# A recurrence beside a full attention: the new memory turned on VectorE instead of TensorE, its inputs loaded as tokens, the five instruction orders set anew

## The chip, the cores and the metric

The kernel runs on one core of one Trainium2 chip. The metric is the device time of one execution in microseconds; three runs of the kernel before gave 1315.05, 1323.09 and 1323.85 us, with a median of 1323.09 us. One more execution was profiled, and all durations come from it.

## The reference

Two attentions over the same kind of input are mixed by a gate. Part A is a recurrence over 64 segments of 32 tokens: each segment is preceded by 8 memory rows, and the first 8 rows of its output are the memory of the next segment. Part B is ordinary softmax attention with 32 heads of 18 elements over 2048 tokens.

```python
for s in range(n_seg):                       # 64 segments, one after the other
    xs = x[:, s * seg_len:(s + 1) * seg_len, :]
    h = jnp.concatenate([mem, xs], axis=1)   # 8 + 32 rows of 576
    q, k, v = (einsum('btd,dhe->bhte', h, W) for W in (Wq, Wk, Wv))   # 32 heads of 128
    p = softmax(where(mask, q @ k^T * scale, -1e9))
    o = einsum('bhte,hed->btd', p @ v, Wo)
    mem = o[:, :M, :]                        # M = 8
    outs.append(o[:, M:, :])
# b = softmax attention of B_x with wqkv and wo;  g = sigmoid((x * gate_w).sum(-1))
out = g * a + (1 - g) * b
```

B_x is given, but the mix uses A_x for both parts.

## The kernel before, in words

**How the work is laid out.** The kernel lists some 8,600 operations with `add(name, engines, cost, function, dependencies, ...)`; each function issues a handful of instructions. The order of the operations on each engine is written out by hand in `ORDER` (L16): one list for each of TensorE (PE), VectorE (DVE), ScalarE (ACT), GpSimd (POOL) and SyncE (SP), as steps from one operation's number to the next. Every engine works through its list strictly in order. `FULL` (L309) names the products that run untiled where two forms are possible. `Plan.run` (L424) only merges the five lists into one program with the help of the costs, and picks zero products (below).

**Stages.** First x is transposed on TensorE (`xt`, L717) into xT, and the projections of part B follow (`pq` L870, `pv` L908), while the weights of part A are loaded from the POOL queue (L807, L812). Then two things run interleaved until the end. Part B is 512 visits: a visit is four row-tiled score products (`sb`, L1065), two exponentials on ScalarE (L1074, L1078) and four column-tiled value products (`ob`, L1088). Part A is the 64 segments: projections Q, K, V (L1437, six results of four chunks each, and a tail that two results share, `T`), evictions on VectorE (32x32 block transposes L1478, casts L660), copies into `qk` and `v_sb` on POOL or VectorE (L1522, L1502), scores (L1544), exponential (L1554), sums and their reciprocals (L1570, L1582, L1590), the weighted values (`po`, L1612), evictions into `ot`, and the output product in two halves (`op0`, `op1`, L1319). Queries, keys and values of the last 8 tokens of each segment don't depend on the memory and are made ahead (`la`, L1156 and L1160, stores `ls`). At the end the output product of part B (`pfx`, L1831) and the gate's mix follow.

**From one segment to the next.** Half 0 of the output product is summed on VectorE (L1346). When half 1 is done, VectorE adds the two into `obf` as 128 partitions by 144 columns, bfloat16 (`oc`, L1645). TensorE turns the memory rows of it by 16 small products with slices of the identity (`fo`, L1660 and L1667), and VectorE copies the result into columns 0 to 7 of `ht` (`ph`, L1676). The other 24 columns of `ht` are the segment's tokens: POOL copies them (`lh`, L1386) from `xg`, which is loaded for four segments at a time (`lx`, L1380) from `xtd`, a copy of xT in DRAM stored once (`xs`, L835). The projections of the next segment wait for both copies. Features stand in `ht` as four chunks of 128 rows and a fifth with the 4 x 16 left over; the weights are loaded in the same order of rows (`row0`, `rows`).

**Zero products.** Between the first and the last value product of a visit group the planner looks at how long TensorE would wait for its next operation. From about 0.3 us on it puts four zero-weight products of 512 columns there (or one untiled), which add nothing to the open accumulator (`warm_col`, `warm_full`, L1036 and L1042).

**Banks and tokens.** The value accumulator `ob` has a PSUM bank of its own and `sb` three; four more (`pb`) are handed round between all others, the fourth score product of a visit, the projections, `acc` of the output product and `pw` of the turned memory among them.

Of the kernel before, what the change touches and what calls it, by code (L numbers as in the profile page):

```python
# [1898 lines left out]
```

## Time and profile before

| | |
|---|---|
| median of 3 runs | 1323.09 us |
| profiled execution, its time | 1319.63 us |
| profiled execution, span of the instructions | 1317.8 us |
| instructions | 72973 |
| HBM read, written | 52.74 MB, 31.12 MB |
| projections of part B end | at about 95 us |
| first segment's projections start | at about 128 us |

Engines in the page: PE is TensorE's products, PEld its weight loads, DVE VectorE, ACT ScalarE, POOL GpSimd, SP the queue of DMA issues. A group's row has the line, engine, operation, output and input tiles, shape and count, then busy us and mean ns of one, then the idle time ahead of it and what ended that. Products are pipelined, so a row's duration is longer than its distance to the next: the distance between starts tells what TensorE really spent.

### The profile page before, as it was taken

Reading aid. Unit: us, or ns where it says so; the run is one execution under the profiler, and the core shown is the slowest. Engines: PE = TensorE matmul, PEld = TensorE weight load, DVE = VectorE, ACT = ScalarE, POOL = GpSimd, SP = SyncE. Lnnn points to the kernel's source line nnn. Section 1 sums busy time; section 2 is a strip of 40 time slices with the busy share of each in tenths; the row PEclk is TensorE's granted clock in tenths of the full one; section 3 lists DMA queues with packets and bytes.
Section 4 is the critical chain, followed back from the end, with each engine's and each line's share of the span. In section 5 each row is a group of like instructions: output and inputs, shape, how many; then the busy total and the mean of one; then the engine's idle time right before and its main releaser. Section 6 shows DMA issues by size and latency. Waiting matters only on the chain.

```text
span 1317.8 us, 72973 instructions
## 1 busy us (share of the span) xinstructions
PE 1287.2 (98%) x32799; PEld 692.9 (53%) x32799; DVE 781.2 (59%) x1778; ACT 1118.5 (85%) x1343; POOL 519.2 (39%) x1291
## 2 busy tenths in 40 slices
PE   8999999999999999999999999999999999999998
PEld 5444544555555555555555545655555444544555
DVE  3234566656566666565656666656666566566667
ACT  3678989978889898888978898898878899998896
POOL 4361353423543246434452445543334343423320
PEclk9999999999999999999999999999999999999999
DMA  8887522011211021111121211121122111111115
GB/s 240 273 287 243 176 48 49 26 31 28 64 40 42 16 47 53 31 31 36 41 49 30 43 38 39 34 49 30 36 49 63 25 23 24 35 38 25 22 51 184
DMA packets 145063, 88.59 MB, mean 67 GB/s; under 512 B 102439, under 2 KB 135383, under 8 KB 144751
## 3 DMA queue, kind: packets, MB, share of 16 engines
q1 hardware_dynamic: 127527, 51.33, 15.2%
q0 software_dynamic: 15088, 30.41, 7.6%
q8 instruction: 256, 4.19, 1.3%
q10 hardware_dynamic: 2136, 2.19, 0.6%
q14 instruction: 56, 0.46, 0.1%
HBM read 52.74 MB, written 31.12 MB: 64 GB/s over the span
## 4 chain that ended last, share of the span: by engine, by line
PE 88%; ACT 4%; DMA 3%; DVE 2%; issue 2%; SPq 1%; DVEq 0%; ACTq 0%
PE pvv L1437 31%; PE acc L1319 12%; PE sb L1065 12%; PE ob L1088 9%; PE pv L1156 5%; PE pso L1612 3%; ACT etb L1074 3%; PE pv L1160 3%; PE pq L870 2%; PE psh L1544 2%; PE prb L1590 2%; PE po L1831 1%; PE psh L1536 1%; PE pw L1660 1%; PE pvb L908 1%
## 5 line engine op out<-in xcount | busy, mean ns | idle before, releaser
L1074 ACT ACTIVATE etb<-sb 128x1536 bf16<-128x1536 f32 x512 | 744.0, 1453 | 118.8 <-PE sp L1065 89.5
L1078 ACT ACTIVATE etb<-sp 128x512 bf16<-128x512 f32 x512 | 306.5, 599 | 0.8 <-PE sp L1065 0.7
L1437 PEld LDWEIGHTS <-ht 128*32 128x32 bf16 (+1 forms) x7680 | 170.6, 94 | 215.4 <-issue 115.8
L1478 DVE STREAM_TRANSPOSE tf<-pvv 128x512 f32<-128x512 f32 x256 | 181.2, 714 | 166.0 <-PE pvv L1437 159.5
L1522 POOL CAST qk<-tf 128x512 bf16<-128x512 f32 x142 | 88.0, 621 | 342.9 <-DVE tf L1478 339.8
L1502 POOL COPY v_sb<-tm 32x256 f32<-32x256 f32 x360 | 147.9, 411 | 153.7 <-DVE tm L660 103.0
L1065 PE MATMUL sb<-qch,kch 32*128 32x512 bf16 x1536 | 202.0, 385 | 5.0 <-ACT etb L1074 1.9
L1065 PE MATMUL sp<-qch,kch 32*128 32x512 bf16 x512 | 196.6, 384 | 2.0 <-DVE vt L660 1.8
L1088 PE MATMUL ob<-etb,vch 128*32 128x512 bf16 x2048 | 194.8, 383 | 1.6 <-issue 0.6
L1437 PE MATMUL pvv<-wk_m,ht 128*32 128x512 bf16 x2048 | 163.2, 381 | 0.2
L1437 PE MATMUL pvv<-wq_m,ht 128*32 128x512 bf16 x2048 | 162.7, 381 | 0.7
L1319 PE MATMUL acc<-wo,ot 128*32 128x288 bf16 (+1 forms) x6144 | 160.2, 248 | 1.1 <-DVE ot L660 0.6
L1437 PE MATMUL pvv<-wv_m,ht 128*32 128x512 bf16 x2048 | 155.2, 380 | 0.2
L1319 PEld LDWEIGHTS <-ot 128*32 128x32 bf16 x6144 | 113.5, 97 | 31.3 <-issue 11.4
L1065 PEld LDWEIGHTS <-kch 32*128 32x128 bf16 x2048 | 56.2, 91 | 121.3 <-issue 107.5
L660 DVE CAST ot<-pso 128x320 bf16<-128x320 f32 x192 | 87.7, 485 | 45.8 <-PE pso L1612 43.9
L660 DVE CAST tm<-pvv 128x512 bf16<-128x512 f32 x101 | 69.2, 687 | 45.2 <-PE pvv L1437 41.8
L1088 PEld LDWEIGHTS <-vch 128*32 128x32 bf16 x2048 | 52.0, 95 | 48.2 <-issue 30.9
L1601 DVE TENSOR_TENSOR et<-et,prb 128x320 bf16<-128x320 bf16 x128 | 62.0, 486 | 23.1 <-PE prb L1590 17.5
L1554 ACT ACTIVATE et<-psh 128x320 bf16<-128x320 f32 x128 | 55.7, 440 | 17.6 <-PE psh L1544 16.4
L660 DVE CAST vl<-pv 128x512 bf16<-128x512 f32 x65 | 44.6, 690 | 40.6 <-PE pv L1156 24.2
L1405 POOL COPY qk<-xl 128x64 f32<-128x64 f32 x256 | 52.2, 244 | 28.4 <-DMA xl<-qkd 8.9
(160 smaller groups left out, 1810.6 us busy)
## 6 DMA issues: line engine op xcount, KB each, us to landing
xl<-qkd SPq DMA_DIRECT2D x32, 256.0 KB
qkd<-vl SPq DMA_DIRECT2D x41, 128.0 KB
wo<-in_A_Wo_dram POOLq DMA_DIRECT2D x8, 576.0 KB, 5.8
wq_m<-in_A_Wq_dram POOLq DMA_DIRECT2D x8, 512.0 KB, 6.8
vgd<-vt SPq DMA_DIRECT2D x32, 128.0 KB
wk_m<-in_A_Wk_dram POOLq DMA_DIRECT2D x8, 512.0 KB, 6.8
wv_m<-in_A_Wv_dram POOLq DMA_DIRECT2D x8, 512.0 KB, 5.7
v_sb<-vld SPq DMA_DIRECT2D x128, 32.0 KB
```

The costliest lines, as they stand in the source:

```text
L660: nc.vector.tensor_copy(out=out_of(), in_=in_of())
L1065: nc.tensor.matmul(sb[:, j, :] if j < 3 else sp[:, :], lhsT=kc[r, o:o + P], rhs=qt_[r, :], start=True, stop=True, tile_position=(32 * j, 0),)
L1074: nc.scalar.activation(out=etb[:, 0:3, :], in_=box["sb", gq, kb][:, :, :], func=ACT.Exp, scale=scale_b)
L1078: nc.scalar.activation(out=etb[:, 3, :], in_=box["sp", gq, kb][:, :], func=ACT.Exp, scale=scale_b)
L1088: nc.tensor.matmul(ob[32 * j:32 * j + 32, :], lhsT=vc[:, o + 32 * j:o + 32 * j + 32], rhs=etb[:, j, :], start=(kb == 0), stop=(kb == NKB - ...
L1156: nc.tensor.matmul(out_, lhsT=lw, rhs=rw, start=(c == 0), stop=(c == NF), skip_group_check=wide)
L1319: nc.tensor.matmul(acc[32 * q:32 * q + 32, :], lhsT=o[:, slot, t0:t0 + CT], rhs=wo[:, h, d:d + n], start=(first and s_ == (s_ % 2 if wide ...
L1437: nc.tensor.matmul(o, lhsT=ht[:, c, :], rhs=rw, start=start, stop=stop, tile_position=(r, 32 * j), skip_group_check=True,)
L1478: nc.vector.transpose(out=tf[:, :], in_=box["pvv", s, n][:, :])
L1502: move(out=out_.bitcast(FP32), in_=in_.bitcast(FP32)) if e == "POOL" else move(out=out_, in_=in_)
L1522: move(out=opened["qk"][:, hf, a, 0:16 * L].rearrange("p (k t) -> p k t", t=L)[:, :, 0:CT], in_=box["tf", s, "QK"[a] + str(hf)][:, :].rear ...
L1601: nc.vector.tensor_tensor(out=et[:, :], in0=et[:, :], in1=box["prb", s, hf][:, :], op=ALU.mult)
```

## The change

It does five things.

1. The fold on TensorE (`fo`) and the copy behind it (`ph`) are gone. While half 1 of the output product runs, VectorE prepares `gs`: the summed half 0, multiplied by a mask that keeps the 8 memory rows, plus the next segment's tokens. After half 1, `gx` multiplies the accumulator by the same mask and adds the prepared rows, into `hn` (128 x 144, bfloat16). `gt` turns columns 0 to 127 of `hn` into `ht` by 32x32 blocks; `gc` (two copies) and `gv` do the same for the 16 left over. `oc` follows `gx`. The four main chunks of a projection wait for `gt`, the shared tails for `gv`.
2. Tokens are loaded as they are, one row of the input after the other (`lx`, four DMAs for four segments, straight from x), into the rows of `xg` where the mask is zero. `xtd`, its stores `xs` and the copies `lh` are gone.
3. The order of features follows from that: row 32g + r of chunk c is feature 144g + 32c + r. x is transposed in 20 column-tiled pieces instead of 5 untiled ones, and weights, gate and tails are loaded in that order; a weight load moves 2048 columns of a row at once, where it moved two pieces of 1024.
4. The zero products are gone, and so is the planner's model of instruction fetches that went with them.
5. `ORDER` and `FULL` are written anew for all engines, and some costs that the planner uses are changed.

The lists themselves, read as operation numbers, hold: TensorE 4501 operations before and 4437 after, VectorE 1684 and 2038, ScalarE 1358 and 1257, POOL 680 and 728, SP 374 and 259.

```diff
 ORDER = {
...
-    LAG = {"SP": 0.66, "ACT": 0.66, "POOL": 1.25}
+    LAGS = ({"SP": 0.8, "ACT": 0.8, "POOL": 2.5}, {"SP": 0.66, "ACT": 0.66, "POOL": 1.25})
...
-    def zeros(self, op, est, mode):
...
     def rows(t, c):
-        return t[row0(c):row0(c) + P, :]
+        return t.rearrange("(g r) n -> g r n", r=RW)[:, 32 * c:32 * c + 32, :]
...
-            for c in range(NF):
-                nc.tensor.transpose(out=ptx[:, c, :], in_=xn[:, row0(c):row0(c) + P], identity=ident[:, :])
...
+            for c in range(NF + 1):
+                for g in range(4):
+                    r = slice(32 * g, 32 * g + 32)
+                    lw = xn[:, RW * g + 32 * c:RW * g + 32 * c + 32] if c < NF else xd[:, r]
+                    nc.tensor.transpose(out=ptx[r, c, :], in_=lw, identity=ident[:, :], tile_position=(0, 32 * g))
...
-    xstores = [store_xt(q) for q in range(NQC)]
...
+    def later_x(s):
+        def ld_x(e):
+            src = x_td[s * seg:(s + 4) * seg, :].rearrange("(i t) d -> t i d", t=seg)
+            for g in range(NF):
+                queue(e)(out=opened["xg"][32 * g + M:32 * g + CT, :, :], in_=src[0:seg - LO, :, RW * g:RW * g + RW])
+
+        return add(f"lx{s}", *carrier(4, s > 0), ld_x, [opening, last_x], dmas=4, kb=110)
+
+    def turned_state(s, deps, state, held):
+        def merge(e):
...
+                nc.vector.scalar_tensor_tensor(
+                    out=hn[:, 0:RW], in0=state["acc"][:, :], scalar=opened["mrow"][:, 0:1], in1=held()[:, RW:2 * RW],
+                    op0=ALU.mult, op1=ALU.add,
+                )
+
+        def swap(e):
+            hn = opened["hn"]
+            for k in range(2):
+                nc.vector.tensor_copy(out=hn[64 * k:64 * k + 64, RW:RW + TR], in_=hn[64 - 64 * k:128 - 64 * k, P:RW])
+
+        def flip(a, b):
+            def fn(e):
+                ht = opened["ht", s % 2][:, :, :].rearrange("p c t -> p (c t)")
+                nc.vector.transpose(out=ht[:, a:b], in_=opened["hn"][:, a:b])
+            return fn
+
+        used = hist.get(s - 2, {}).get("used", ())
+        gx = add(f"gx{s}", "DVE", 0.37, merge, deps)
+        gt = add(f"gt{s}", "DVE", 0.22, flip(0, P), [gx, *used])
+        gc = add(f"gc{s}", "DVE", 0.16, swap, [gx])
+        return gx, gt, add(f"gv{s}", "DVE", 0.11, flip(P, P + 32), [gc, *used])
...
-                        [ops[0]] if c else [h_ready, lh, *weight_loads[("wq", "wk", "wv")[kind]]],
+                        [ops[0]] if c else [h_main, *weight_loads[("wq", "wk", "wv")[kind]]],
...
-            both = add(f"T{names[0]}.{s}", "PE", 0.216, tails, [ops[0] for ops in parts], mode="quad", pairs=8)
+            both = add(f"T{names[0]}.{s}", "PE", 0.216, tails, [h_tail, *(ops[0] for ops in parts)], mode="quad", pairs=8)
...
+            def prepare(e, s=s, st0=first_half):
+                nc.vector.scalar_tensor_tensor(
+                    out=st0["sum"][:, RW:2 * RW], in0=st0["sum"][:, 0:RW], scalar=opened["mrow"][:, 0:1],
+                    in1=opened["xg"][:, (s + 1) % 4, :], op0=ALU.mult, op1=ALU.add,
+                )
...
+        c1 = add(f"oc{s}", "DVE", 0.308, ob_cast, [mids[1], half_sum, nxt], take=("obf",) if s % 4 == 0 else (),
...
-            fo = add(f"fo{s}", "PE", 0.13, fold, [c1], mode="col", take=("pb",), pairs=16, drain=0.245)
...
-            h_ready = add(f"ph{s}", "DVE", psum_copy(40), put_h, [fo, *prev.get("used", ())], give=(("pb", fo, 0),))
```

More of the change, by code (lines that the diff above doesn't have):

```diff
@@ L463, in run @@
                 mode = op.form
-                open_ = (open_ or op in self.opens) and op not in self.closes
-                self.count += op.waits
-                dur += self.fetched(est, dur, pairs)
             op.eng, op.start, op.end = e, est, est + dur
@@ L570 @@
     nc.vector.memset(veil[:], 0.0)
-    nil = const.tile([P, P], BF16, name="nil")
-    nc.vector.memset(nil[:], 0.0)
     nc.vector.memset(bsel[:], 0.0)
@@ L587 @@
     )
-    selm = ident[:, :].rearrange("p (a b t) -> p b a t", a=2, t=32)[:, :, :, 0:M]
-    SL = (0, 2, 1, 3)
     dpool = ctx.enter_context(tc.tile_pool(name="dpool", bufs=1, space=bass.MemoryType.DRAM))
     a_dram = dpool.tile([S, Dm], BF16, name="a_dram")
-    xtd = dpool.tile([(NF + 1) * P, S], BF16, name="xtd")
     qtd = dpool.tile([Dm, S], BF16, name="qtd")
@@ L712, in dup @@
         def dup(e):
-            box["xd", n] = xd = given(pw, "xd", [P, 2, 2, 2 * TR], BF16)
-            tail = box["xn", n][:, :].rearrange("p (b r) -> p b r", r=2 * RW)[:, :, P:P + 2 * TR]
-            nc.vector.tensor_copy(out=xd[:, :, :, :], in_=tail.unsqueeze(1).to_broadcast([P, 2, 2, 2 * TR]))
-        du = add(f"xd{n}", "DVE", 0.2, dup, [ld], take=("xd",))
+            box["xd", n] = xd = given(pw, "xd", [P, 2, 2, 2, TR], BF16)
+            tail = box["xn", n][:, :].rearrange("p (h g r) -> p g h r", h=2, r=RW)[:, :, :, P:RW]
+            nc.vector.tensor_copy(out=xd[:, 0, :, :, :], in_=tail)
+            for h in range(2):
+                nc.vector.tensor_copy(out=xd[:, 1, :, 1 - h, :], in_=tail[:, :, h, :])
+        du = add(f"xd{n}", "DVE", 0.3, dup, [ld], take=("xd",))
         def turn(e):
@@ L1032 @@
     last_vi = last_va = None
-    def warm_col(e):
-        for j in range(4):
-            nc.tensor.matmul(
-                box["ob"][32 * j:32 * j + 32, :], lhsT=nil[:, 0:32], rhs=ident[:, :].unsqueeze(1).to_broadcast([P, 4, P]), start=False, stop=False,
-                tile_position=(0, 32 * j), skip_group_check=True,
-            )
-    def warm_full(e):
-        nc.tensor.matmul(
-            box["ob"][:, :], lhsT=nil[:, :], rhs=ident[:, :].unsqueeze(1).to_broadcast([P, 4, P]),
-            start=False, stop=False, skip_group_check=True,
-        )
-    plan.warm = {"col": warm_col, "full": warm_full}
     for gq in range(GB * NQC):
@@ L1227, with first_mem @@
     opened = {}
+    def first_mem():
+        return opened["ot"][:, :, :].rearrange("p h t -> p (h t)")[:, 0:RW]
     def open_rest(e):
@@ L1262, in load_m0 @@
     def load_m0(e):
-        m0 = opened["ot"][:, :, :].rearrange("p h t -> p (h t)")[:, 0:Dm]
-        dma(out=m0[0:M, :], in_=A_mem0[0])
-        box["m0"] = m0
-    m1 = add("m0", "SP", 0.4, load_m0, [opening], dmas=1, kb=10)
-    def dup_m0(e):
-        m0d = opened["et", 0][:, 0:P].rearrange("p (a b r) -> p a b r", a=2, b=2)
-        tail = box["m0"][0:M, :].rearrange("p (b r) -> p b r", r=2 * RW)[:, :, P:P + 2 * TR]
-        nc.vector.tensor_copy(out=m0d[0:M, :, :, :], in_=tail.unsqueeze(1).to_broadcast([M, 2, 2, 2 * TR]))
-        box["m0d"] = m0d
-    m2 = add("m0d", "DVE", 0.25, dup_m0, [m1])
-    def turn_m0(e):
-        ptm = bank([P, NF + 1, 32], BF16, "ptm")
-        for c in range(NF):
-            nc.tensor.transpose(
-                out=ptm[:, c, 0:M], in_=box["m0"][0:M, row0(c):row0(c) + P], identity=ident[0:M, 0:M]
-            )
-        nc.tensor.transpose(
-            out=ptm[:, NF, 0:M], in_=box["m0d"][0:M, :, :, :].rearrange("p a b r -> p (a b r)"),
-            identity=ident[0:M, 0:M],
-        )
-        box["ptm"] = ptm
-    m3 = add("m0t", "PE", 0.3, turn_m0, [m2], mode="full", take=("pb",), pairs=5)
-    def put_m0(e):
-        ht, ptm = opened["ht", 0], box["ptm"]
-        nc.vector.tensor_copy(out=ht[:, :, 0:M], in_=ptm[:, :, 0:M])
-    h_ready = add("m0h", "DVE", 0.55, put_m0, [m3], give=(("pb", m3, 0),))
+        for g in range(NF):
+            dma(out=first_mem()[32 * g:32 * g + M, :], in_=A_mem0[0][:, RW * g:RW * g + RW])
+    m0 = add("m0", "SP", 1.6, load_m0, [opening], dmas=4, kb=10)
     plan.tokens_of("tm", 2)
@@ L1302 @@
     plan.tokens_of("tf", 2)
-    plan.tokens_of("xg", 1)
     a_stores = {}
@@ L1374 @@
         ht_i = s % 2
-        if s % 4 == 0:
-            def ld_x(e, s=s):
-                box["xg", s // 4] = xg = given(opened["fix"], "xg", [P, NF + 1, P], BF16)
-                src = slice(s * seg, (s + 4) * seg)
-                queue(e)(out=xg[:, :, :], in_=xtd[:, src].rearrange("(c p) t -> p c t", p=P))
-            lx = add(f"lx{s}", *carrier(1, s > 0), ld_x, [opening, xstores[s * seg // QC], prev.get("lh")], take=("xg",), dmas=1, kb=164)
-        def put_x(e, s=s, ht_i=ht_i):
-            ht, xg, t = opened["ht", ht_i], box["xg", s // 4], slice(s % 4 * seg, s % 4 * seg + seg - LO)
-            nc.gpsimd.tensor_copy(out=ht[:, :, M:CT].bitcast(FP32), in_=xg[:, :, t].bitcast(FP32))
-        lh = add(f"lh{s}", "POOL", 0.24, put_x, [lx, *prev2.get("used", ())], give=(("xg", lx, 0),) if s % 4 == 3 else ())
-        cur["lh"] = lh
+        if s == 0:
+            lx = later_x(0)
+            _, h_main, h_tail = turned_state(0, [m0, lx], None, None)
         def ld_l(e, s=s, sq=sq, si=si):
@@ L1508 @@
             pvs.append((
-                add(f"qd{hf}.{s}", ("DVE", "POOL"), (0.8, 0.75), put_v(hf, (1, 3)), before),
-                add(f"qc{hf}.{s}", ("DVE", "POOL"), (0.8, 0.75), put_v(hf, (0, 2)), before),
+                add(f"qd{hf}.{s}", ("DVE", "POOL"), (0.71, 0.87), put_v(hf, (1, 3)), before),
+                add(f"qc{hf}.{s}", ("DVE", "POOL"), (0.71, 0.87), put_v(hf, (0, 2)), before),
             ))
@@ L1527 @@
                 turned.append(add(
-                    f"ct{a}{hf}.{s}", ("POOL", "DVE"), (0.66, 0.45), ct, [ev_a, prev.get(f"psh{hf}")], give=(("tf", ev_a, 0),),
+                    f"ct{a}{hf}.{s}", ("POOL", "DVE"), (0.63, 0.435), ct, [ev_a, prev.get(f"psh{hf}")], give=(("tf", ev_a, 0),),
                 ))
@@ L1574, in sm @@
                         )
-            s_ = add(f"sm{hf}.{s}", "PE", 0.08, sm, [x_],
-                     mode="col", take=("pb",), pairs=12, alt=("full", 0.088, 3), drain=0.218)
+            s_ = add(f"sm{hf}.{s}", "PE", 0.1, sm, [x_],
+                     mode="col", take=("pb",), pairs=12, alt=("full", 0.11, 3), drain=0.218)
             def rc(e, hf=hf, s=s):
@@ L1616, in pso @@
                         )
-            o_ = add(f"po{hf}.{s}", "PE", 0.2, pso, [n_, lv, *pvx], mode="tall", take=("pb", "pb"), pairs=16, waits=0.15, drain=0.26,
+            o_ = add(f"po{hf}.{s}", "PE", 0.25, pso, [n_, lv, *pvx], mode="tall", take=("pb", "pb"), pairs=16, waits=0.15, drain=0.26,
                      give=(("tm", evx, 0),))
@@ L1645, in ob_cast @@
             nc.vector.tensor_tensor(
-                out=opened["obf"][:, s % 4, TR:TR + RW], in0=st["acc"][:, :], in1=st0["sum"][:, 0:RW], op=ALU.add
+                out=opened["obf"][:, s % 4, :], in0=st["acc"][:, :], in1=st0["sum"][:, 0:RW], op=ALU.add
             )
-        c1 = add(f"oc{s}", "DVE", 0.308, ob_cast, [mids[1], half_sum], take=("obf",) if s % 4 == 0 else (),
+        nxt = None
+        if s + 1 < n_seg:
+            def prepare(e, s=s, st0=first_half):
[3 more added lines that the diff above has]
+                )
+            if (s + 1) % 4 == 0:
+                lx = later_x(s + 1)
+            gs = add(f"gs{s + 1}", "DVE", 0.27, prepare, [half_sum, lx])
+            nxt, h_main, h_tail = turned_state(s + 1, [mids[1], gs], acc_state, lambda st0=first_half: st0["sum"])
+            last_x = gs
+        c1 = add(f"oc{s}", "DVE", 0.308, ob_cast, [mids[1], half_sum, nxt], take=("obf",) if s % 4 == 0 else (),
                  give=(("pb", acc_state["op0"], 0), ("sum", sum_op, 0)))
@@ L1685, in st_a @@
                     queue(e)(
-                        out=dst[0:seg - LO, :, RW * SL[j]:RW * SL[j] + RW],
-                        in_=opened["obf"][32 * j + M:32 * j + CT, :, TR:TR + RW],
+                        out=dst[0:seg - LO, :, RW * j:RW * j + RW], in_=opened["obf"][32 * j + M:32 * j + CT, :, :],
                     )
@@ L1818, in mul_a @@
                     nc.vector.tensor_scalar_mul(out=ga_view(n), in0=ares_all[:, n, :], scalar1=gsb[:, n:n + 1])
-            gates[n] = add(f"ga{n}", ("ACT", "DVE"), (act_time(576), 0.65), mul_a, [la, *last["used"]])
+            gates[n] = add(f"ga{n}", ("ACT", "DVE"), (0.77, 0.51), mul_a, [la, *last["used"]])
     HD2 = Dm // 2
@@ L1851 @@
             halves.append(add(
-                f"cb{n}.{hf}", "DVE", psum_copy(288), combine, [a, gates[n]], give=(("pb", a, 0),)
+                f"cb{n}.{hf}", "DVE", 0.518, combine, [a, gates[n]], give=(("pb", a, 0),)
             ))
```

150 lines of the change are left out of this document (51 added, 99 removed), and 583 rows, old and new, of tables (FULL, ORDER).

## The prediction

> **What bounds the kernel now.** I read the page first: busy shares and the chain that ended last.
>
> ```profile
> span 1317.8 us, 72973 instructions
> ...
> PE 1287.2 (98%) x32799; PEld 692.9 (53%) x32799; DVE 781.2 (59%) x1778; ACT 1118.5 (85%) x1343; POOL 519.2 (39%) x1291
> ...
> PE 88%; ACT 4%; DMA 3%; DVE 2%; issue 2%; SPq 1%; DVEq 0%; ACTq 0%
> ```
>
> TensorE is the bound: 98% busy, 88% of the chain. But a product's row is longer than its distance to the next, so that share hides short waits. What TensorE spends must be read from the starts, in the timeline. I took the passage from one segment to the next, because the change sits there; this one is typical.
>
> ```profile
> 402.36 0.30 DVE L1346 TENSOR_TENSOR sum<-acc,sum 64x144 f32<-64x144 f32 x1
> 402.38 0.61 PE L1319 MATMUL acc<-wo,ot 128*32 128x144 bf16 x28
> ...
> 402.81 0.39 PE L1088 MATMUL ob<-etb,vch 128*32 128x512 bf16 x4
> ...
> 403.03 0.39 PE L1036 MATMUL ob<-ident,nil 128*32 128x512 bf16 x4
> 403.04 0.31 DVE L1645 TENSOR_TENSOR obf<-acc,sum 128x144 bf16<-128x144 f32 x1 [0.38 <-PE acc L1319]
> ...
> 403.41 0.22 PE L1660 MATMUL pw<-ident,obf 128*32 128x16 bf16 x8
> ...
> 403.47 0.20 PE L1667 MATMUL pw<-ident,obf 128*32 128x8 bf16 x8
> ...
> 403.61 0.39 PE L1065 MATMUL sb<-qch,kch 32*128 32x512 bf16 x3
> ...
> 403.75 0.20 DVE L1676 CAST ht<-pw 128x40 bf16<-128x40 f32 x1 [0.40 <-PE pw L1667]
> ...
> 403.93 0.43 PE L1088 MATMUL ob<-etb,vch 128*32 128x512 bf16 x4
> ...
> 404.15 1.07 PE L1437 MATMUL pvv<-wv_m,ht 128*32 128x512 bf16 x16
> ```
>
> Prices from these starts. Four column products of 512 take 0.22 us (402.81 to 403.03). The same work followed by another tiling costs more: `sb` at 403.61 to `ob` at 403.93 is 0.32, so **a change of tiling costs 0.10 us**. The fold takes 0.20 up to `sb`, of which 0.10 is such a change: 0.10 of its own. The zero products take 0.22, and TensorE waits another 0.16 for the fold (403.03 to 403.41, less 0.22). The seven rounds of `acc` are 0.0625 apart, so the last starts at 402.76 and the next segment's projections 1.39 later. Read alike for all 63 passages the mean is 1.45 us, 91.4 us in sum: 51.0 useful products, 12.2 changes of tiling, 6.6 fold, 5.0 zero products (23 of them lie here) and **16.6 us of waits**, 8.8 of them just ahead of the fold. The groups agree:
>
> ```profile
> L1660 PE MATMUL pw<-ident,obf 128*32 128x16 bf16 x504 | 14.4, 176 | 1.1 <-issue 0.5 <-DVE obf L1645 0.5
> L1036 PE MATMUL ob<-ident,nil 128*32 128x512 bf16 x212 | 20.2, 379 | 0.0
> L1042 PE MATMUL ob<-ident,nil 128*128 128x512 bf16 x4 | 1.2, 379 | 0.0
> L1660 PEld LDWEIGHTS <-obf 128*32 128x32 bf16 x504 | 8.7, 94 | 23.5 <-DVE obf L1645 21.8 <-issue 0.8
> ...
> PEld L1660 <- DVE obf L1645: 21.8, 53, 0.7
> ```
>
> 504 is 63 folds of 8; 212/4 + 4 makes 57 zero products. The fold's weight loads waited 21.8 us in 53 cases for VectorE's sum; less the 0.22 that the product ahead was still streaming, that is 10 us, close to 8.8.
>
> **The passage after the change.** The chain is now `acc`, `gx`, `gt`, projections. `gx` and `gt` are not in the trace; the nearest rows:
>
> ```profile
> L1645 DVE TENSOR_TENSOR obf<-acc,sum 128x144 bf16<-128x144 f32 x64 | 19.7, 308 | 33.1 <-PE acc L1319 31.6 <-DMA kch<-ktd 1.2
> L1846 DVE SCALAR_TENSOR_TENSOR wk_m<-po,omg,wv_m 128x288 bf16<-128x288 f32 x24 | 12.2, 516 | 2.4 <-PE po L1831 1.1 <-PE po L1835 0.2
> L1131 DVE STREAM_TRANSPOSE stage<-tn 128x512 bf16<-128x512 bf16 x32 | 22.3, 696 | 1.9 <-DMA otd<-stage 1.7
> L660 DVE CAST ot<-pso 128x320 bf16<-128x320 f32 x192 | 87.7, 485 | 45.8 <-PE pso L1612 43.9
> L660 DVE CAST tm<-pvv 128x512 bf16<-128x512 f32 x101 | 69.2, 687 | 45.2 <-PE pvv L1437 41.8
> L1676 DVE CAST ht<-pw 128x40 bf16<-128x40 f32 x63 | 12.5, 199 | 28.4 <-PE pw L1667 28.4
> ```
>
> The two casts give 1.05 ns per column ((687-485)/192). By that `gx` is 516 - 144 x 1.05 = 0.365 us; its bounds are 0.31 (a plain sum of that size) and 0.52 (the 288 columns). `gt` is 696 - 384 x 1.05 = 0.29; its bounds are 0.17 (a quarter of 696) and 0.49 (a cast of 320 columns). I take the slope, because L1676 shows that even 40 columns cost 0.20. The sum of VectorE starts 0.28 after the last `acc` round (403.04 - 402.76), and the least time seen from `ph` to the projections is 0.055, where no product stood between. So the chain is 0.28 + 0.365 + 0.29 + 0.055 = 0.99 us, with 0.82 to 1.35 at the bounds. The new TensorE list has 2.9 operations in the passage (36 of 63 times `ob ob sb`) where 3.4 useful ones stood: 0.06 + 2.9 x 0.22 + two changes of tiling = 0.90 us. The longer of both sets the passage: 0.99, or 0.90 to 1.35. 63 x 0.99 = 62.4 us; 0.5 operations each, 6.6 us, are done elsewhere. **Saved: 91.4 - 62.4 - 6.6 = 22.4 us** (28 down to 0). The fold and its share of zero products are in that.
>
> **The rest, step by step.**
>
> *Orders.* From the diff's lists I counted TensorE's changes of tiling: 1566 before, 1508 after. 58 x 0.10 = **5.8 us saved**; in the passages there are about two each time in both, so these lie elsewhere. The visits are dealt out to the segments almost as before (7 or 8 each), so it is the same plan locally rearranged. What rearranging does to the remaining waits the trace can't say; the page shows 1317.8 - 1287.2 = 30.6 us of plain idle time, and I bound it by a third of that, 10 us either way, and take 0.
>
> *Zero products elsewhere.* 34 x 0.22 = 7.5 us of TensorE time, put where it would have waited anyway. Only the overshoot is gained: I take 1, bounds 0 and 7.5.
>
> *Early stage.*
>
> ```profile
> xtd<-xT SPq DMA_DIRECT2D x4, 640.0 KB
> ...
> 70.00:80.00 10.00, 7.71 (x46) 3.44 (x47) 2.67 (x9) 4.94 (x6) 3.18 (x7) 0.83 1.01 348
> ...
> L1240 POOL MEMSET v_sb<- 128x1024 f32 x1 | 1.0, 951 | 10.7 <-DMA xtd<-xT 10.7
> ```
>
> Four stores of 640 KB vanish; POOL waited 10.7 us for them before it opened the recurrence's buffers. TensorE is short of work only at 70 to 80 us, 2.3 us of it, with the DMA engines full. The 20 column pieces of a transposed tile stream in five rounds, as the five untiled ones did: nothing. I take **2 us saved**, bounds 0 and 4.
>
> *VectorE and ScalarE.* Each segment adds `gs` (like `gx`, 0.365), `gx`, `gt`, two small copies of `gc` and `gv` (0.20 each at most, by L1676), and drops `ph`: 1.42 us, 63 times 89 us. The new lists also move evictions from ScalarE to VectorE, by the fall of ScalarE's list 101, some 60 of them in the recurrence, at 0.49 to 0.69 us: 55 us. VectorE comes to 781 + 89 + 55 = 925 us, 70%. `gs` hides in the time in which VectorE waits for `acc` (L1645: 31.6 us idle there). Behind `gx` and `gt`, the tails of `gc` and `gv` are hidden under eight main chunks (1.7 us), and `oc`, which frees `acc`, comes some 0.6 us later than before; the bank of `pw`, held about as long, is no longer taken. ScalarE is relieved of about as many evictions, and 4% of the chain is ScalarE's. I charge **5 us lost** for results that come late in a fuller queue; bounds: 10 lost, 5 gained.
>
> *SyncE and POOL.* The lists move 321 DMA issues to POOL (`lq`, `lk`, `lv`, `fs`, `ls`, `sa`, `so`, and `lx` with four issues). POOL's `lh` goes.
>
> ```profile
> L985 POOL DMA_DIRECT2D qch<-qtd x64 | 32.7, 518 | 1.1 <-PE sp L1065 0.7 <-issue 0.4
> L1386 POOL COPY ht<-xg 128x60 f32<-128x60 f32 x64 | 14.9, 235 | 12.5 <-PE pvv L1437 7.3 <-DMA xg<-xtd 2.3 <-issue 1.6
> POOL qk L1522 <- DVE tf L1478: 339.8, 113, 12.0
> ```
>
> 321 x 0.52 - 15 = 152 us more, 671 us or 51%. POOL waited 340 us for VectorE ahead of its casts, so there is room: 0.
>
> **Sum.** 22.4 + 5.8 + 1 + 2 - 5 = 26 us. The profiled execution took 1319.6 us (span 1317.8), 3.5 under the median of 1323.1. 1319.6 - 26 = **1294 us**. The likeliest case itself reaches from 1283 to 1308.
>
> **Rivals.**
>
> *The gain is eaten.* `gx` and `gt` come at their upper bounds, half of the passage's gain is lost (11), and the new order gives 8 back in waits: 1319.6 - 11 - 5.8 + 8 = 1311 us. For it: nothing in the trace shows a 128-column transpose. Against: two independent rows lie on the slope.
>
> *More is gained.* The chain hides wholly under `ob ob sb` (28), all zero products count (7.5), the early stage gives 4, late results cost nothing: 1319.6 - 28 - 5.8 - 7.5 - 4 = 1274 us.
>
> *Slower: POOL's queue.* About 65 more bursts of four issues, 2.1 us each, stand in the queue that also casts `qk` for the scores. If a burst stands ahead of a cast that is due, the segment waits for it. 65 x 0.65 us (a third of a burst) is 42 us: 1294 + 42 = 1336. It decides from 0.4 us per burst on, where the gain is gone. Against: the 340 us of idle time above, in which POOL stands ready early.
>
> [...]
>
> *The clock.* Without zero products TensorE might be throttled in the gaps.
>
> ```profile
> 271.37 0.33 PE L1590 MATMUL prb<-ident,rq 107*32 107x107 bf16 x12 [2.45 <-DVE vl L660]
> ...
> 250.00:300.00 50.00, 47.45 (x1288) 25.79 (x1278) 26.55 (x57) 41.56 (x50) 14.72 (x41) 0.97 0.13 32
> ```
>
> In the recurrence the granted clock fell once, around the 2.45 us gap, and cost 3% of 50 us, 1.5 us. If each of the 34 places outside the passages did that: 1294 + 51 = 1345 us. Against: the zero products filled 0.3 to 0.9 us, and a lone gap of that size left the clock at 1.
>
> **How the numbers follow.** The forecast has 0.46, the eaten gain 0.24, more gain 0.14, POOL 0.11, the clock 0.05. 1% of 1323 is 13 us, about what a measurement can tell: faster is below 1310. Faster: 0.43 + 0.08 + 0.14 = 0.65; within 1%: 0.03 + 0.16 and 0.05 of mild forms of the last two, 0.24; slower 0.11. The range from 1274 to 1328 leaves out the outer ends of three rivals, about 0.18.
>
> **What would show it.** Right: no L1660 and L1667 rows; the passage from the last `acc` round to the projections at about 1.0 us; a transpose of 128 columns at 0.29 and a sum with mask at 0.365; VectorE near 925 us, POOL near 670, ScalarE some 50 lower; clock at 1 from 100 us on. Wrong: passages above 1.3 us; TensorE's weight loads waiting for POOL's `qk` casts or for `kch`, `qch`, `vch`; windows with a clock under 0.97.

## The result, and the profile after

The changed kernel takes **1395.3 us** (median of 4 runs, 1393.1 to 1398.8) against 1321.4 before in the same comparison: 1.057 times as long, 95% interval 1.052 to 1.061. Forecast were 1294 us, faster. Neither the size nor the sign was right.

The page of the changed kernel: its span, the engines' busy time, the chain by engine.

```profile
span 1397.0 us, 75359 instructions
...
PE 1283.8 (92%) x33859; PEld 679.3 (49%) x33880; DVE 907.4 (65%) x2214; ACT 1074.3 (77%) x1242; POOL 684.8 (49%) x1568
...
PE 68%; DVE 10%; DMA 9%; issue 6%; ACT 4%; POOL 1%; SPq 1%; DVEq 0%; ACTq 0%; POOLq 0%
```

TensorE is busy for as long as before, in a span 79 us longer: it fell from 98% to 92%, so it waits. In the chain DMA rose from 3 to 9%, "issue" (no wait that the profile shows) from 2 to 6%, VectorE from 2 to 10%. To find where, I cut the span at two marks that both traces have: the sum that ends segment 0 (`oc`), and that of segment 63. Before, they start at 162.7 and 1291.6 us, after at 204.9 and 1371.8. So **42.2 us are lost ahead of segment 0's memory, 38.0 between the marks** (1128.9 to 1166.9), and 1.0 is gained behind.

The early part, in stretches of 50 us, before and then after (columns: stretch and length, busy time of PE, PEld, DVE, ACT, POOL with instructions, granted clock, DMA share, GB/s):

```profile
0.00:50.00 50.00, 43.79 (x343) 26.16 (x344) 14.69 (x70) 21.44 (x39) 22.87 (x65) 0.97 0.83 251
50.00:100.00 50.00, 47.55 (x375) 22.00 (x374) 15.68 (x46) 39.74 (x49) 24.20 (x56) 0.96 0.87 283
```

```profile
0.00:50.00 50.00, 30.44 (x421) 16.69 (x426) 20.63 (x101) 5.34 (x8) 10.43 (x29) 0.93 0.50 144
50.00:100.00 50.00, 37.67 (x281) 17.92 (x282) 16.49 (x44) 14.87 (x18) 19.24 (x49) 0.86 0.83 191
```

In the first 50 us the DMA engines carry 144 GB/s at half load, where they carried 251 at 0.83. All compute engines except VectorE do less. The granted clock is lower too, in stretches in which TensorE is busy for 30 and 38 of 50 us; which of the two causes the other these rows don't show. The changed kernel's chain through its first 60 us names what it waits for (start, us, what). First the one wait for `wb` in the chain of the kernel before, then the two of the changed kernel:

```profile
4.33 2.75 DMA wb<-in_B_wqkv_dram
```

```profile
5.00 14.41 DMA wb<-in_B_wqkv_dram
19.43 8.16 DMA wb<-in_B_wqkv_dram
```

One load of 144 KB takes 14.4 us there. A's weight loads became slower as well (last column: median us from issue to landing), first before and then after:

```profile
wq_m<-in_A_Wq_dram POOLq DMA_DIRECT2D x8, 512.0 KB, 6.8
wk_m<-in_A_Wk_dram POOLq DMA_DIRECT2D x8, 512.0 KB, 6.8
wv_m<-in_A_Wv_dram POOLq DMA_DIRECT2D x8, 512.0 KB, 5.7
```

```profile
wq_m<-in_A_Wq_dram POOLq DMA_DIRECT2D x8, 512.0 KB, 11.7
wk_m<-in_A_Wk_dram POOLq DMA_DIRECT2D x8, 512.0 KB, 13.7
wv_m<-in_A_Wv_dram POOLq DMA_DIRECT2D x8, 512.0 KB, 12.3
```

The bytes are the same. What changed is the form: in the new row order a load's outermost dimension is 4 groups, where it was 128 rows. The record of single DMA packets shows the difference. During those 14.4 us (5.0 to 19.4) exactly four packets were under way for 48% of the time, and 6.0 in the mean. Before the change, exactly four were under way for less than 1% of the same stretch, and the mean was 13.9. The DMA share in it was 0.87 before and 0.37 after.

Between the marks, I added up the distances between the starts of TensorE's products (us). "Streaming" is what the columns need; "inside" is what is over between two products of one operation that wait for nothing.

| | streaming | changes of tiling | at an operation's start | inside an operation |
|---|---|---|---|---|
| before | 920.9 | 141.4 | 49.1 | 17.2 |
| after | 906.4 | 134.8 | 69.5 | 56.0 |
| difference | -14.5 | -6.6 | +20.4 | **+38.8** |

They sum to +38.1. Gaps over 40 ns inside operations went from 4.2 us to 42.7; these are called stalls below. The longest, in the timeline of the changed kernel:

```profile
918.09 0.41 PE L1091 MATMUL pv<-xL,wk_m 128*32 128x128 bf16 x16
...
918.25 0.10 PEld L1091 LDWEIGHTS <-wk_t 128*32 128x32 bf16 x1
...
920.57 0.24 PE L1091 MATMUL pv<-xL,wk_t 128*32 128x128 bf16 x4 [2.07 <-issue]
920.57 0.10 PEld L1091 LDWEIGHTS <-wk_t 128*32 128x32 bf16 x3 [2.21 <-issue]
```

One of four weight loads is made, then nothing for 2.2 us, then the other three. No semaphore lies between them. The instructions themselves were missing:

```profile
q8 instruction: 265, 4.34, 1.3%
```

265 packets on this queue, for 33,859 products and 33,880 weight loads: 67,739 / 256 = 264.6, so a packet of 16 KB brings 256 of TensorE's instructions, 128 pairs. (Before: 65,598 / 256 = 256.2, and 256 packets.) In the record of this queue one packet starts at 918.25, 2.3 us ahead of the resumption. So it is for all 37 stalls over 0.3 us: TensorE resumed 2.3 to 2.9 us after a packet's start. The closest two of these packets start 3.30 us apart in the trace before and 3.34 in the trace after. **Here a stretch that goes on using up 128 pairs in much less than that waits for its own instructions.** The last units' Q and K pieces, in column form, are such a stretch; the groups show how many more there are, first before and then after:

```profile
L1156 PE MATMUL pv<-xL,wk_m 128*128 128x128 bf16 x352 | 29.5, 220 | 0.1
...
L1160 PE MATMUL pv<-xL,wk_m 128*32 128x128 bf16 x640 | 14.5, 219 | 0.0
```

```profile
L1091 PE MATMUL pv<-xL,wk_m 128*32 128x128 bf16 x1424 | 33.8, 220 | 8.0 <-issue 7.9
...
L1087 PE MATMUL pv<-xL,wk_m 128*128 128x128 bf16 x156 | 12.5, 220 | 0.0
```

A piece is 5 products in full form (128*128) or 20 small ones in column form (128*32), with the same result. Over Q and K together, 65 of 192 pieces were in column form before; it is 180 now. Ahead of the stall above, pieces of twenty pairs start 0.28 us apart, so 128 pairs take 1.8.

The passage between segments, which the change was about, did get shorter. A typical one:

```profile
660.68 0.86 PE L1233 MATMUL acc<-wo,ot 128*32 128x144 bf16 x44
...
661.25 0.37 DVE L1595 SCALAR_TENSOR_TENSOR sum<-sum,mrow,xg 128x144 f32<-128x144 f32 x1
...
661.37 0.60 PE L1023 MATMUL ob<-etb,vch 128*32 128x512 bf16 x8
...
661.73 0.37 DVE L1300 SCALAR_TENSOR_TENSOR hn<-acc,mrow,sum 128x144 bf16<-128x144 f32 x1
...
661.90 0.39 PE L1000 MATMUL sb<-qch,kch 32*128 32x512 bf16 x3
...
662.13 0.31 DVE L1313 STREAM_TRANSPOSE ht<-hn 128x128 bf16<-128x128 bf16 x1
...
662.49 0.40 PE L1380 MATMUL pvv<-wk_m,ht 128*32 128x512 bf16 x4 [0.20 <-DVE ht L1313]
```

The last `acc` round starts at 661.31, the projections 1.18 later: TensorE waits 0.20 for the transpose. The row at 661.25 is `gs`; it ends at 661.62, and `gx`, which needs its result, starts at 661.73. The mean over 63 passages is 1.18 us, 74.6 in sum, where it was 1.45 and 91.4.

### The profile page after: what moved, and what is told of

Read it like the earlier page. It is cut to its first block, busy times and chain, and to the rows that moved or that the text cites. A ratio compares the mean times of both kernels' runs of the same rounds, so it can differ in the third digit from the quotient of the medians.

```text
span 1397.0 us, 75359 instructions
## 1 busy us (share of the span) xinstructions
PE 1283.8 (92%) x33859; PEld 679.3 (49%) x33880; DVE 907.4 (65%) x2214; ACT 1074.3 (77%) x1242; POOL 684.8 (49%) x1568
## 4 chain that ended last, share of the span: by engine, by line
PE 68%; DVE 10%; DMA 9%; issue 6%; ACT 4%; POOL 1%; SPq 1%; DVEq 0%; ACTq 0%; POOLq 0%
PE pvv L1380 28%; PE sb L1000 8%; PE acc L1233 8%; PE ob L1023 6%; PE pv L1091 5%; DMA vch<-vgd 3%; ACT etb L1009 3%; PE pso L1555 3%; PE pv L1087 2%; PE psh L1487 2%; DMA wb<-in_B_wqkv_dram 2%; DVE hn L1300 1%; DVE ot L622 1%; PE psh L1479 1%; PE prb L1533 1%
## 5 line engine op out<-in xcount | busy, mean ns | idle before, releaser
L1380 PEld LDWEIGHTS <-ht 128*32 128x32 bf16 (+1 forms) x7680 | 167.2, 94 | 249.4 <-issue 105.9
L1445 POOL COPY v_sb<-tm 32x256 f32<-32x256 f32 x388 | 159.5, 411 | 123.6 <-DVE tm L622 98.7
L1000 PE MATMUL sb<-qch,kch 32*128 32x512 bf16 x1536 | 203.5, 387 | 14.4 <-DMA kch<-ktd 6.0
L1465 POOL CAST qk<-tf 128x512 bf16<-128x512 f32 x128 | 81.2, 638 | 193.7 <-DVE tf L1421 186.5
L1380 PE MATMUL pvv<-wq_m,ht 128*32 128x512 bf16 x2048 | 168.5, 381 | 4.8 <-DVE ht L1313 3.1
L1380 PE MATMUL pvv<-wk_m,ht 128*32 128x512 bf16 x2048 | 167.5, 381 | 3.8 <-DVE ht L1313 1.9
L1233 PE MATMUL acc<-wo,ot 128*32 128x288 bf16 (+1 forms) x6144 | 163.6, 250 | 4.1 <-issue 2.2
L622 DVE CAST ot<-pso 128x320 bf16<-128x320 f32 x215 | 97.2, 484 | 57.1 <-PE pso L1555 51.5
L622 DVE CAST tm<-pvv 128x512 bf16<-128x512 f32 x122 | 83.5, 688 | 52.8 <-PE pvv L1380 51.5
L1544 DVE TENSOR_TENSOR et<-et,prb 128x320 bf16<-128x320 bf16 x128 | 61.8, 485 | 30.6 <-PE prb L1533 24.5
L622 DVE CAST vl<-pv 128x512 bf16<-128x512 f32 x75 | 51.2, 687 | 40.9 <-PE pv L1087 23.7
L935 POOL DMA_DIRECT2D qch<-qtd x116 | 59.1, 516 | 16.4 <-issue 5.6
## 6 DMA issues: line engine op xcount, KB each, us to landing
wq_m<-in_A_Wq_dram POOLq DMA_DIRECT2D x8, 512.0 KB, 11.7
wk_m<-in_A_Wk_dram POOLq DMA_DIRECT2D x8, 512.0 KB, 13.7
wv_m<-in_A_Wv_dram POOLq DMA_DIRECT2D x8, 512.0 KB, 12.3
```

Of the source, the lines that this page charges most:

```text
L622: nc.vector.tensor_copy(out=out_of(), in_=in_of())
L1000: nc.tensor.matmul(sb[:, j, :] if j < 3 else sp[:, :], lhsT=kc[r, o:o + P], rhs=qt_[r, :], start=True, stop=True, tile_position=(32 * j, 0),)
L1233: nc.tensor.matmul(out_, lhsT=o[:, slot, t0:t0 + CT], rhs=rw, start=(first and s_ == (s_ % 2 if wide else 0)), stop=(last and s_ == (14 + ...
L1380: nc.tensor.matmul(o, lhsT=ht[:, c, :], rhs=rw, start=start, stop=stop, tile_position=(r, 32 * j), skip_group_check=True,)
L1445: move(out=out_.bitcast(FP32), in_=in_.bitcast(FP32)) if e == "POOL" else move(out=out_, in_=in_)
L1465: move(out=opened["qk"][:, hf, a, 0:16 * L].rearrange("p (k t) -> p k t", t=L)[:, :, 0:CT], in_=box["tf", s, "QK"[a] + str(hf)][:, :].rear ...
```

## The experiments

Two theories: **A**, the early loss comes from the loads' form; **B**, the recurrence's loss comes from the fetching of TensorE's instructions. Their rival is that both are signs of something else: later results on VectorE and POOL, the column-form transposes of x, the new orders.

| run | us | ratio to before [95%] | segment 0's memory at | between the marks | stalls |
|---|---|---|---|---|---|
| after | 1395.3 | 1.057 [1.052, 1.061] | 204.9 | 1166.9 | 42.7 |
| wb16 | 1383.8 | 1.049 [1.046, 1.052] | 187.2 | 1169.8 | 40.5 |
| all16 | 1371.7 | 1.038 [1.034, 1.043] | 172.8 | 1175.0 | 45.7 |
| qkfull | 1357.0 | 1.028 [1.024, 1.033] | 196.7 | 1129.1 | 4.4 |
| both | 1335.7 | 1.013 [1.009, 1.016] | 170.5 | 1136.3 | 5.5 |
| rows4 | 1357.3 | 1.028 [1.024, 1.033] | 201.1 | 1123.2 | 4.2 |
| small | 1361.0 | 1.029 [1.024, 1.033] | 158.7 | 1165.3 | 33.6 |
| nozeros | 1323.3 | 1.001 [0.999, 1.004] | 160.3 | 1131.8 | 5.8 |
| oldorder | 1345.6 | 1.019 [1.016, 1.023] | 187.5 | 1130.6 | 6.7 |
| tuned | 1327.8 | 1.006 [1.003, 1.008] | 179.4 | 1119.0 | 2.0 |
| tuned2 | 1335.7 | 1.012 [1.009, 1.015] | 178.3 | 1128.5 | 3.7 |
| part32 | 1324.9 | 1.003 [1.001, 1.006] | 167.2 | 1125.5 | 5.0 |
| split4 | 1313.3 | 0.9967 [0.9939, 0.9995] | 168.8 | 1116.0 | 3.6 |

The kernel before stood at 1319 to 1322 us in each comparison. The last three columns come from one profiled execution of each kernel. Between the marks before, rows4 and part32 do the same work in the same order and differ by up to 5.8 us, after, wb16 and all16 by up to 8.1: smaller differences there mean little.

**wb16 and all16: another form of the same loads.** First `wb` alone, from 4 groups x 32 rows to 32 rows x 4 chunks:

```diff
-out=wb[:, c, cols], in_=rows(B_wqkv, c)[:, :, cols]
+out=wb[32 * c:32 * c + 32, 0:NF, cols], in_=block_rows(B_wqkv, c)[:, :, cols]
+    def block_rows(t, g):
+        return t[RW * g:RW * g + P, :].rearrange("(c r) n -> r c n", r=32)
```

> The changed kernel with only B's wb loads issued anew: the same 12 transfers of 144 KB, but each fills 32 partitions x 4 chunks (outermost dimension 32 rows) in place of 4 groups x 32 rows (outermost dimension 4), and the two tail loads are split in halves of 16 rows. Theory A (the early loss of 42 us comes from transfers whose outermost dimension is 4, so that they spread over few DMA engines): wb lands in some 4 to 6 us where it took 14.4, the first score round comes near 45 us where it was 70.5, segment 0's memory some 25 us sooner than 204.9, and the time falls to about 1370 us; the rest of the 42 us stays, since A's weights still load in the old form. Rival (the input's column-form transposes, 20 products in place of 5, and the new orders cost the early stage): under 5 us gained, 1390 or more.

then A's weights as well, in the same way:

> As the run before, and the 24 loads of A's weights (512 KB each) in the same way: 32 partitions x 4 chunks, outermost dimension 32. Theory A: a weight load lands in about 6 us as before the change (11.7 to 13.7 with it), segment 0's memory comes near 165 us in place of 204.9, and the time falls by some 40 us to about 1355. Rival (orders and transposes): the early stage keeps most of its 42 us, 1385 or more.

11.5 and 23.6 us came back, less than expected both times (the expected times were about 1370 and 1355). In wb16's chain the longest wait for `wb` was 5.9 us. In the first two stretches of 50 us the DMA share was 0.83 and 0.97 in wb16, 0.92 and 1.01 in all16, and 0.50 and 0.83 after the change. Segment 0's memory moved from 204.9 to 187.2 and 172.8, 32 of the 42 us; between the marks they were 3 and 8 us longer than the changed kernel. So A is right in kind and held for three quarters of the early loss. Weight loads landed in these times, still above those of before:

```profile
wq_m<-in_A_Wq_dram POOLq DMA_DIRECT2D x8, 512.0 KB, 7.5
wk_m<-in_A_Wk_dram POOLq DMA_DIRECT2D x8, 512.0 KB, 10.0
wv_m<-in_A_Wv_dram POOLq DMA_DIRECT2D x8, 512.0 KB, 7.0
```

**qkfull and both: fewer pairs.**

```diff
-alt=None if not q else ("full", 0.216, 1) if kind == 2 else ("col", 0.279, 20), drain=0.2,
+alt=("full", 0.216, 1) if q and kind == 2 else None, drain=0.2,
```

> The changed kernel with the last units' Q and K products always in the full form (5 products in place of 20 small ones; 180 such pieces of 20 become 5, so 2700 fewer product pairs), at the price of some 105 more changes of tiling at 0.10 us. Theory B (the recurrence's loss of 38 us is TensorE waiting for its own instructions: a block of 256 instructions, 128 pairs, can't be followed by the next sooner than some 3.6 us): the stalls inside an operation without a wait fall from 42.7 us to under 12, the changes give back 10, and the time falls by 20 to 30 us to about 1370. Rival C (VectorE's queue, or POOL's, is late, and the stalls only show it): the stalls move elsewhere, and the added changes of tiling make it about 1405.

> Both edits together (wb and A's weights over all engines; Q and K pieces in the full form). If A and B are independent causes, the gains add: about 1328 us, near the kernel before. If the early stage hides nothing of it and the rivals hold, 1385 to 1405.

qkfull gained 38 us, more than expected: the stalls fell from 42.7 to 4.4, although changes of tiling cost 10.5 more (134.8 to 145.3). B holds, and rival C falls: nothing on VectorE or POOL was touched. The two edits together gained 59.5, their sum is 61.8, so the two causes add up; the kernel stayed at 1335.7, above the 1328 that was expected.

**small and rows4: the same causes put into the kernel before.**

```diff
-if op.alt and (mode == op.alt[0] or op.seq in FULL):
+if op.alt and (mode == op.alt[0] or op.alt[0] == "col" or op.seq in FULL):
```

> The kernel before with all 192 pieces of the last units' Q and K in the column form of 20 small products (65 of them have it before, 180 in the changed kernel), nothing else altered. Theory B: 127 pieces more of 15 more pairs, 1905 pairs, in dense runs; stalls inside operations rise from 4 us to 35 or 45, and the time to 1350 to 1365 us although changes of tiling get fewer. Rival (fewer changes of tiling are worth 0.10 us each and nothing stands against them, as the prediction took it): 1308 to 1315.

39 us slower, as B expected. The groups of this run, against those of before above:

```profile
L1160 PE MATMUL pv<-xL,wk_m 128*32 128x128 bf16 x1536 | 36.9, 220 | 7.2 <-issue 6.7 <-ACT etb L1078 0.3
```

```diff
-out=wb[:, c, cols], in_=rows(B_wqkv, c)[:, cols]
+out=wb[:, c, cols], in_=rows4(B_wqkv, c)[:, :, cols]
+    def rows4(t, c):
+        return t.rearrange("(g r) n -> g r n", r=RW)[:, 32 * c:32 * c + 32, :]
...
+out=w[0][:, c, half, :].rearrange("p b f -> p (b f)"), in_=rows4(w2, c)[:, :, cols]
```

> The kernel before with its loads of wb and of A's three weights (12 of 144 KB and 24 of 512 KB) read in the changed kernel's form: outermost dimension of 4 groups, 32 rows each, one row long. The rows then lie in another order than x's columns, and A's column blocks as well, so the values computed are others than the reference's; the work on every engine is the same. Theory A: wb lands in 14 us, weights in 12 to 14 us, segment 0's memory comes 32 to 42 us later than 162.7, and the time rises to 1352 to 1362. Rival (order and transposes of the changed early stage): within 5 us of before.

36 us slower, segment 0's memory 38.4 later, weights landing in 10.3 to 12.3 us. From 5.0 to 19.4 us exactly four packets were under way for 38% of the time. So the form of the loads makes nearly all of the early loss by itself. The column-form transposes of x and the new early orders are not needed for it.

**nozeros: the zero products alone.**

```diff
-if e == "PE" and open_:
+if False:
```

> The kernel before without its zero products (57 of them, 10.0 us of streaming between segment 0's memory and the last), all else and every queue as before. The prediction's own term: they stand in waits, so taking them away gives 0 to 7.5 us: 1313 to 1321. Rival of the prediction (the clock drops where TensorE idles): about 1345, with the granted clock below 0.97. Theory B in its sharper form (where the 128-pair blocks end decides what is late, and the hand-set order fits the blocks of before): the ends move by 1 to 4 pairs per product, stalls inside operations come up from 4 us, and the time rises by up to 14 us, 1320 to 1334, at an unchanged clock.

No difference that can be measured (1.001 [0.999, 1.004]), at a clock of 0.997. The stalls hardly moved (4.2 to 5.8), so the sharper form of B was not needed, and the clock rival falls.

**oldorder: the changed operations in the old order.** The lists of the kernel before, with `gx`, `gt`, `gc`, `gv` in front of `oc`, `gs` behind the half-sum, loads as in all16.

> The changed kernel's operations in the order of the kernel before: every operation that both have keeps its place and its form, the merge, the two transposes and the swap stand where VectorE cast the memory, the masked sum right behind the half-sum, x's token loads on GpSimd's queue; loads as in all16, no zero products. Step of the prediction under test: turning on VectorE alone saves 22 us in the passages and costs 5 on VectorE, and the order adds 6: so 1296 to 1306 with the old order. Rival (1.6 us more in line on VectorE per segment, ahead of the evictions that the old order counted on, and the 128-pair blocks fall elsewhere): the passages shorten, yet waits for VectorE and fetch stalls of 10 us or more come up, 1325 to 1345.

Between the marks 1130.6 us, as before (1128.9): the turning gains nothing in an order made for another kernel. Waits ahead of `sb`, the score rounds, rose from 5.5 to 21.0 us, and the passages came to 1.34 us in the mean. Ahead of segment 0's memory it lost 24.8. The prediction's 22 us are not there. The time is at the upper end of the rival's range, but not for the rival's reasons alone: the early loss, which the expectation left out, makes up nearly all of it, and stalls stayed at 6.7. The waits that came up stand ahead of the score rounds; of 13.0 us of TensorE's idle time there between 210 and 1290 us, 10.3 were ended by ScalarE's exponentials (1.0 of 3.0 before), not by VectorE. Why those came later is open.

**tuned and tuned2: the orders set once more.** Both with the loads of all16, each piece's form fixed, and orders searched with blocks of 128 pairs 3.65 us apart in the plan's arithmetic.

> The changed kernel with both causes taken away and its orders set once more: wb and A's weights over all engines as in the run all16, each piece's form written out (no rule that takes the column form whenever it stands next), and the queues' orders searched with the 128-pair blocks (3.65 us apart) and VectorE's durations as the changed kernel's trace has them (0.31 us for the main transpose, 0.35 for the two swaps, 0.20 for the tail, 0.37 for the masked sum). If the prediction's gain is real and was only covered by the two losses (a passage of 1.16 in place of 1.39 us, 11 to 17 us in 63 passages, and some 5 us of waits), it is faster than the kernel before: 1300 to 1312, with stalls inside operations under 6 us and segment 0's memory near 168 us. Rival (the turned memory gives back on VectorE's queue and at the score rounds what the passage saves): 1318 to 1330.

Between the marks it was 1119.0 us, 10 less than before the change, with 2.0 us of stalls. But segment 0's memory came at 179.4, and the whole was 0.6% slower: in time the rival's number, for another reason.

> As the run tuned, with the orders searched on from a slower early loading (the traces of all16 and tuned moved 243 to 250 GB/s between 50 and 100 us with the DMA engines full, where the kernel before moved 283 at 0.87). If the 17 us that tuned lost ahead of segment 0's memory (179.4 against 162.7) are a matter of how the early work is ordered around slower loads, some 8 to 12 of them come back: segment 0's memory near 168 to 171 us, the period stays at 17.75 us, and the time is 1308 to 1318, below the kernel before by up to 1%. Rival: the early stage is bound by the loads themselves however it is ordered, 1322 to 1330.

A miss, above the rival's range too: 1.1 us came back early (178.3), and the recurrence lost its gain (9.5 us). A better order in the search's arithmetic was a worse one on the chip.

**part32 and split4: why the loads stayed slow.** In the record of packets, those of 4096 bytes took 200 to 213 ns (means of the first and the second 50 us) before the change, and 274 to 293 in all16, at 14 to 15 GB/s each in place of 19 to 20. part32 cuts the old loads into groups of 32 partitions:

```diff
-nc.gpsimd.dma_start(
-    out=w[0][:, half, c, :], in_=rows(w2, c)[:, cols].rearrange("p (b f) -> p b f", f=WB)
-)
+for g in range(0, P, 32):
+    nc.gpsimd.dma_start(
+        out=w[0][g:g + 32, half, c, :],
+        in_=rows(w2, c)[g:g + 32, cols].rearrange("p (b f) -> p b f", f=WB),
+    )
```

> The kernel before with each 512 KB load of A's weights cut into four transfers of 32 partitions (32 consecutive rows each, so that all engines still take part, by the outermost dimension of 32), nothing else. Theory P (32 partitions at a time are a slower target than 128, whatever the rows' order; it would explain why all16 came back by 32 of 42 us only): packets of 4096 bytes take 260 to 290 ns, as in all16, in place of 200 to 213, and segment 0's memory comes 5 us or more later than 162.7. Rival (the order of the source's rows is what slows a packet): 200 to 220 ns. GpSimd issues 72 more transfers of about 0.6 us, which the waits of that queue should hold; by itself that should not lengthen a packet.

Packets stayed at 216 to 223 ns: theory P fell as it stood, though segment 0's memory came 4.5 us later. The DMA share in the first two stretches of 50 us was 0.86 and 0.89 (0.83 and 0.87 before). But here four transfers in a row cover all 128 partitions. In all16 half a megabyte goes into 32, often twice in a row. So split4 gives tuned's loads that shape:

```diff
-out=w[0][32 * c:32 * c + 32, :, cols], in_=block_rows(w2, c)[:, :, cols]
+for g in range(NF):
+    d = RW * g + 32 * c
+    nc.gpsimd.dma_start(out=w[0][32 * g:32 * g + 32, c, cols], in_=w2[d:d + 32, cols])
```

> The run tuned with each 512 KB load of A's weights cut into four transfers, one for each group of 32 partitions and one chunk (32 consecutive rows of 4096 bytes), in place of one transfer of 32 partitions x 4 chunks; orders and all else as in tuned. part32 had just such transfers on the old row order and kept packets of 4096 bytes at 216 to 223 ns. Theory Q (what slows the packets in all16 and tuned, 262 to 293 ns, is that half a megabyte goes into the same 32 partitions by one transfer and mostly another by the next): packets fall to 210 to 235 ns, segment 0's memory comes 8 to 14 us sooner than 179.4, and the time is 1312 to 1320, level with the kernel before. Rival (the changed order of the source's rows is slow for itself): packets stay above 255 ns, segment 0's memory stays within 5 us of 179, 1323 to 1332.

The stretches of split4, and then the landing of one of its weights:

```profile
0.00:50.00 50.00, 40.94 (x497) 22.76 (x498) 24.44 (x116) 12.40 (x20) 21.50 (x62) 1.00 0.76 189
50.00:100.00 50.00, 43.31 (x383) 20.29 (x381) 16.66 (x50) 36.41 (x43) 42.82 (x104) 0.97 0.97 286
```

```profile
wk_m<-in_A_Wk_dram POOLq DMA_DIRECT2D x32, 128.0 KB, 4.5
```

Packets of 4096 bytes took 242 ns in the first 50 us (262 in tuned) and 221 in the second (276), where the DMA engines moved 286 GB/s, the rate of before (283). Segment 0's memory came 10.6 us sooner than in tuned. At 1313.3 us this version is just faster than the kernel before, 0.9967 [0.9939, 0.9995], and 82 us faster than the change as it was made. What Q expected came. But the walk through the source changed with the partitions (32 rows one after the other in each transfer, where tuned took rows 32 apart), so which of the two slowed the packets is not separated. The same bytes in smaller pieces for all four groups were faster (221 to 242 ns a packet in place of 262 to 276); why, no run shows.

## Why the prediction was wrong, point by point

**The early stage is the first step that failed.** The prediction gave it "2 us saved"; it lost 42.2. I counted the transposes' rounds and the vanished stores, but of the weights' new row order nothing was costed, although the change states it and the diff shows it: the same bytes, a source with 4 groups outermost. rows4 shows its price alone (38.4 us), all16 takes 32 of it back. I also read TensorE as short of work "only at 70 to 80 us". In the first 10 us it was busy for 4.64, and the chain there runs over a load of `wb` (2.75 us): the loads were a limit already. In the changed kernel the DMA engines stood partly idle while a load was waited for: their share was 0.50 in the first 50 us, and 0.37 in the 14.4 us that 144 KB took, with exactly four packets under way for 48% of those. Which engines they were no row shows, nor why so few packets were under way with 4 groups outermost.

**The orders are the second.** "58 x 0.10 = 5.8 us saved" was right as a size: changes of tiling fell from 141.4 to 134.8 us between the marks. The 0 for rearranging, bounded by 10 either way, was wrong by 38: fewer changes were had by 115 more pieces of 20 pairs. I compared lists of operations and not of instructions, and took no notice that the planner's model of fetches went with the zero products. small shows the price in the kernel before (33.6 us of stalls), and in qkfull, without those pieces, the whole 38 us between the marks are back.

**The passage: right in kind, half in size.** Forecast 0.99 us from the last `acc` round, measured 1.18. The groups:

```profile
L1300 DVE SCALAR_TENSOR_TENSOR hn<-acc,mrow,sum 128x144 bf16<-128x144 f32 x63 | 23.2, 368 | 18.3 <-PE acc L1233 14.3
...
L1313 DVE STREAM_TRANSPOSE ht<-hn 128x128 bf16<-128x128 bf16 x64 | 19.9, 311 | 2.1
```

`gx` took 0.368 (0.365 said), `gt` 0.311 (0.29). The hand-overs were undersized: 0.38 in the mean from the last round to `gx` in place of 0.28, 0.06 between `gx` and `gt` counted as nothing, 0.07 to the projections for 0.055. The first has a cause that the prediction ruled out: "`gs` hides in the time in which VectorE waits for `acc`". In 26 of the 63 passages `gx` starts 0.29 us after the last round, as the sum did before the change. In the other 37 it starts 0.10 to 0.12 us after `gs` ends, and all of the lateness, 6.5 us in sum, lies in these. TensorE's useful products there fell from 51.0 to 45.1 us. So 91.4 - 74.6 - 5.9 = **10.9 us saved where 22.4 were forecast**.

**Where that went.** With the stalls gone (qkfull) the stretch between the marks is as long as before, 1129.1 us. Against before: 16.4 less streaming (10.0 zero products, 6.6 fold), but 3.9 more for changes, and 14.3 more at operations' starts. Of those, waits ahead of projections rose from 3.7 to 21.9 while the fold's 6.5 went, and score rounds rose from 5.5 to 11.0. The chain over VectorE put waits where the fold and the zero products had stood. In split4 the stretch is 1116.0, 12.9 less than before, and more than the 5.8 to 8.1 by which equal work differs there. How much of that is the turning and how much the new search is open, since the old kernel's order was not searched again in the same way.

**The rest.** The 5 us charged to VectorE were right in size, in part by luck: score rounds waited 5.5 more in qkfull, but the largest part of the idle time ahead of them was ended by ScalarE's exponentials (2.5 of 5.4 us between 210 and 1290 us). VectorE came to 907 us for 925, ScalarE to 44 less for 50. The 1 us for the zero products is too small to be seen in nozeros (1.001). POOL came to 685 us for 671, and its rival did not come: TensorE's weight loads waited 4.4 us in all for POOL's casts and copies. The clock: between the marks the granted clock dipped once before and four times after, each time to half for 3.4 us; that is 1.7 and 6.8 us, far from the 51 of that rival. Of the listed signs of being wrong, "passages above 1.3 us" did not show in the mean, though 13 of the 63 were above; windows with a clock under 0.97 did show, at 0.93, 0.86 and 0.90 in the first 150 us, while TensorE waited for loads. A load's landing time and the stalls, which did go wrong, were not on the list.

## What to carry to other kernels

Where a change alters the layout of what is loaded, write down for each transfer its outermost dimension and the partitions it fills, before anything on the compute engines is costed (here 4 groups in place of 128 rows, and 11.7 to 13.7 us for 512 KB in place of 5.7 to 6.8). Count instructions as well as operations: a cheaper form with four times the instructions must be checked against the pace at which the engine is supplied (in the traces before and after, 128 pairs in no less than 3.3 us). An order found with one set of limits stays good only while the limits stay in it.
